# B's q by seven products per pair of row blocks, woven with B's k, with some bf16 sums on GpSimd

## The chip, the core and the metric

The kernel runs on one core of a Trainium2 chip. The core has TensorE (matrix products, PE in the profile; its weight loads are listed as PEld), VectorE (DVE), ScalarE (ACT), GpSimd (POOL) and SyncE (SP, which here issues the transfers). All work on SBUF, 128 partitions wide; TensorE writes to PSUM, whose banks serve as accumulators and hold 512 fp32 columns each. The metric is the device time of one execution in microseconds, here as the median of three runs: 192.18 us before.

## What is computed

Two linear-attention blocks, A and B, with their own weights, are applied to the same x and mixed by a gate of x. x is 2048 rows of 640 features, there are 32 heads of 20 features, everything is bf16.

```python
phi = lambda t: jnp.where(t > 0, t + 1, jnp.exp(t)) + 1e-6

def _A_ref(x, wqkv, wo):            # _B_ref is the same
    q, k, v = ...                   # x @ wqkv, split into heads
    pq, pk = phi(q), phi(k)
    kv = jnp.einsum("bhsd,bhse->bhde", pk, v)
    z = jnp.einsum("bhsd->bhd", pk)
    num = jnp.einsum("bhqd,bhde->bhqe", pq, kv)
    den = jnp.einsum("bhqd,bhd->bhq", pq, z)[..., None] + 1e-6
    return ... (num / den) @ wo

x = A_x
g = _sigmoid((x * gate_w).sum(-1, keepdims=True))
return g * _A_ref(x, A_wqkv, A_wo) + (1 - g) * _B_ref(x, B_wqkv, B_wo)
```

## The kernel before

Features are handled in five chunks of 128 (`DT`), rows in sixteen tiles of 128 (`ST`). `xn` holds x with rows on the partitions, `xT` x transposed; `pk` is phi(k) by rows, `pqT` phi(q) by features.

- **k.** `k_chunk` (L213) makes one row tile of phi(k): ten products of 320 columns into one accumulator of two banks (L205), then `phi` (L192): ScalarE takes the exponential (L195), VectorE clamps it in SBUF (L198) and takes the maximum with t + 1, read from the accumulator (L202).
- **q.** `q_unit` (L248) makes one feature chunk for 1024 rows: two times five products of 512 columns (L254), then `phi` on 1024 columns. With `lifted`, ScalarE also writes t + 1 to SBUF (L197), so that VectorE's maximum reads bf16 from SBUF only (L200).
- **G = x^T phi(k).** The fifth chunk of features runs directly (`g_pass`, L276, products at L288). The other four are done by seven products on 2 x 2 blocks (Strassen) in `g_strassen` (L320, products at L315). The sums of blocks that this needs are made by VectorE (`x_sum`, `k_sum`, all through L454).
- **KVT, M.** `kvt_pass` (L409) makes v's part from G, masked by head; `m_unit` (L417) multiplies it by wo, chunk by chunk, into `M`.
- **z and the denominators.** `z_rows` (L364) sums phi(k) over the rows, `z_pass` (L381) selects heads, `rec_pass` (L435) makes the gated reciprocals, `norm_spread` (L485) spreads them, and `scale` (L501) multiplies `pqT` with them.
- **Output.** pqT_A M_A + pqT_B M_B, again by seven products, for pairs of row tiles (`Pair`, L525, products at L515). VectorE makes the sums of blocks: `p_diff` (L456) writes D3, `p_sums` (L461) and `m_sums` (L472) the others, one line of `q_pass` makes TM0, the difference of M_A's halves.

The stages follow one another: A's k and q, A's G, B's k with A's KVT between, B's q, B's G, output. From the first G on, each engine works in the order in which the code is written (`tc.manual_schedule`); TensorE's first part is ordered by a planner. `ps` hands out four accumulators of two banks each in turn (`turn`), so a unit's accumulator is asked for again by the fourth unit after it. B's part stands in these lines:

```python
for i in range(ST):
    k_chunk(1, i)
    if i == 1:
        kvt_pass(0)
        wv[1] = load_w(1, "v", nc.sync)
    if i in (3, 6, 9, 12):
        r0 = (i - 3) // 3 * RB
        p_diff(slice(r0, r0 + RB))
...
zsel = q_pass(1, [(m, h) for h in range(2) for m in range(DT)])
load_wo(1, nc.sync)
g_all(1, zsel)
```

In `q_pass(1, ...)` z's rows, M's five units for A, two differences of k (`k_sum(1, 1)` and `k_sum(1, 2)`) and TM0 stand between the ten q units. GpSimd only builds masks and an identity in the first 10 us.

Of the kernel before, what the change touches and what calls it, by code (L numbers as in the profile page):

```python
# [8 lines left out]
P = 128  # L9
FP32 = mybir.dt.float32  # L10
# [21 lines left out]
def kernel(  # L32
# [19 lines left out]
    banks = ctx.enter_context(ExitStack())  # L52
    psum = banks.enter_context(tc.tile_pool(name="psum", bufs=1, space=bass.MemoryType.PSUM))

    turn = [0]

    def ps_raw(name, slot=None):

        if slot is None:
            slot = turn[0]  # L60
            turn[0] = (slot + 1) % 4
        return psum.tile([P, 4 * HB], BF16, tag=f"ps{slot}", name=name)
# [18 lines left out]
    R = persist.tile([P, 2, 4, RB], BF16, name="R")  # L81
    ones = persist.tile([P, H], BF16, name="ones")
    gwr = persist.tile([P, DT, H], BF16, name="gwr")
    D3 = persist.tile([P, DT, SH], BF16, name="D3")
# [6 lines left out]
    S3 = persist.tile([P, 3, hc, ic], BF16, name="S3")  # L91
    SX = {k: S3[:, k - 1] for k in (1, 2, 3)}
# [3 lines left out]
    lift = persist.tile([P, 1], FP32, name="lift")  # L96
    TM = [persist.tile([P, DT, HF], BF16, name="TM0")] + [None] * 3
    ge = [persist.tile([P, 2 * RB], FP32, name=f"ge{b}") for b in "AB"]
# [93 lines left out]
    def phi(dst, src, n, lifted=False):  # L192

        e = work.tile([P, 2, n], BF16, tag="e", name="e", bufs=3)
        nc.scalar.activation(out=e[:], in_=src, func=ACT.Exp)  # L195
        if lifted:
            nc.scalar.activation(out=dst, in_=src, func=ACT.Identity, bias=lift[:])  # L197
        nc.vector.tensor_scalar(e[:], e[:], 1.0, EPS, op0=ALU.min, op1=ALU.add)  # L198
        if lifted:
            nc.vector.tensor_tensor(out=dst, in0=dst, in1=e[:], op=ALU.max)  # L200
            return
        nc.vector.scalar_tensor_tensor(out=dst, in0=src, scalar=1.0 + EPS, in1=e[:], op0=ALU.add, op1=ALU.max)  # L202
# [7 lines left out]
    def k_done(b, i, pt):  # L210
        phi(pk[:, i, :].rearrange("p (b n) -> p b n", b=2), pt[:, :, 0:HF], HF)
# [36 lines left out]
    def q_unit(b, m, h, lifted=False):  # L248

        pt = ps(f"q{'AB'[b]}")  # L250
        for u in range(2):
            for c in range(DT):
                n = 2 * h + u
                nc.tensor.matmul(  # L254
                    pt[:, u, :], lhsT=mixed(wq[b][:, c, :], m), rhs=xT[:, c, n * HB:(n + 1) * HB],
                    start=(c == 0), stop=(c == DT - 1),
                )
        phi(pqT[b][:, m, h * 2 * HB:(h + 1) * 2 * HB].rearrange("p (b n) -> p b n", b=2), pt, HB, lifted)

    def q_block(b, m, n):  # L260

        pt = ps(f"q{'AB'[b]}")
        for u in range(2):
            for c in range(DT):
                nc.tensor.matmul(  # L265
                    pt[:, u, :], lhsT=mixed(wq[b][:, c, :], m + u), rhs=xT[:, c, n * HB:(n + 1) * HB],
                    start=(c == 0), stop=(c == DT - 1),
                )
        phi(pqT[b][:, m:m + 2, n * HB:(n + 1) * HB], pt, HB)
# [94 lines left out]
    def z_rows(b):  # L364

        pt = ps(f"z{'AB'[b]}")
# [7 lines left out]
        zr = work.tile([P, D], BF16, tag="zr", name="zr")  # L374
# [6 lines left out]
    def z_pass(b, zr):  # L381

        pt = ps(f"zs{'AB'[b]}")
# [8 lines left out]
    def kvt_mm(b, pt, hf):  # L392

        for j in range(4):
            for c in range(DT):
                nc.tensor.matmul(  # L396
                    pt[:KG, hf, j * KG:(j + 1) * KG], lhsT=wv[b][:, c, (4 * hf + j) * KG:(4 * hf + j + 1) * KG],
                    rhs=GT[hf][:, c, j * KG:(j + 1) * KG], start=(c == 0), stop=(c == DT - 1),
                )

    def kvt_mask(pt, hf):

        nc.vector.tensor_tensor(
            out=KVT[:KG, 2 * hf:2 * hf + 2, 0:3:2, :],
            in0=pt[:KG, hf, 0:HF].rearrange("p (g k n) -> p g k n", g=2, k=2),
            in1=maskE[:KG, None, None, :].to_broadcast([KG, 2, 2, KG]), op=ALU.mult,
        )

    def kvt_pass(b):  # L409

        pt = ps("kvA")
        for hf in range(2):
            kvt_mm(b, pt, hf)
        for hf in range(2):
            kvt_mask(pt, hf)
# [40 lines left out]
    def p_diff(rows):  # L456

        up = slice(SH + rows.start, SH + rows.stop)
        add_rows(D3[:, :, rows], pqT[0][:, :, rows], pqT[0][:, :, up], ALU.subtract)

# [64 lines left out]
    class Pair:  # L525
# [13 lines left out]
        def p1(self):  # L539
            prod(self.at("x"), pqT[0][:, :, 0:SH], M[0][:, :, 0:HF], self.i, True)  # L540
            self.p1s = work.tile([P, HF], FP32, tag="e", name="p1s", bufs=3)
            nc.scalar.copy(out=self.p1s[:], in_=self.at("x"))
# [12 lines left out]
        def p6(self):  # L555
            prod(self.at("x"), xT[:, :, 0:SH], TM[1], self.i, False)
            self.u2 = tmp("u2", "ex")
            nc.scalar.copy(out=self.u2[:], in_=self.at("x"))  # L558
            self.u3 = tmp("u3", "zr")
            out_add(self.u3[:], self.at("y"), self.u2[:])  # L560
# [39 lines left out]
    def q_pass(b, units):  # L600

        units = list(units)
        q_unit(b, *units.pop(0))
        if b == 0:
            gate_pass()
        zr = z_rows(b)
        if b == 1:
            m_unit(0, 0, "act")
        for k in range(2):
            if b == 0:  # L610
                x_sum(1 + k)
            q_unit(b, *units.pop(0), b == 0)
        zsel = z_pass(b, zr)
        for k, (m, h) in enumerate(units):
            if b == 0 and k < 2:
                if k:
                    x_sum(3)
                else:
                    k_sum(0, 2)
            q_unit(b, m, h, b == 0)  # L620
            if b == 1 and k in (0, 2):
                for c in range(k + 1, k + 3):
                    m_unit(0, c, "act")
            if b == 1 and k == 0:
                k_sum(1, 1)
            if b == 1 and k == 4:
                add_rows(TM[0][:], M[0][:, :, HF:D], M[0][:, :, 0:HF], ALU.subtract)
        if b == 1:
            k_sum(1, 2)
        return zsel  # L630

    def g_all(b, zsel):

        g_pass(b, DT - 1, 1)
        k_sum(b, 3)
        g_strassen(b, zsel)

# [3 lines left out]
    turn[0] = 2  # L641
    for n in range(2):
        for i in range(CB if n else 0, CB * 2 * n):
            k_chunk(0, i)
        for m in (0, 2):
            q_block(0, m, n)
    q_unit(0, DT - 1, 0)
    for i in range(hc, ST - 2):
        k_chunk(0, i)
# [10 lines left out]
    def late_pool(name):  # L660
        return tc.tile_pool(name=name, bufs=1, space=bass.MemoryType.PSUM, reuse_waits="tile")

# [3 lines left out]
    with tc.manual_schedule():  # L666
# [5 lines left out]
        zsel = q_pass(0, [(m, 1) for m in range(DT)])  # L672
        wq[1] = load_w(1, "q", nc.sync)
        g_all(0, zsel)

        turn[0] = 3
        for i in range(ST):
            k_chunk(1, i)
            if i == 1:
                kvt_pass(0)  # L680
                wv[1] = load_w(1, "v", nc.sync)
            if i in (3, 6, 9, 12):
                r0 = (i - 3) // 3 * RB
                p_diff(slice(r0, r0 + RB))
        t1 = wpool.tile([P, hc, HF], BF16, tag="wk", name="T1")
        TK[1][1] = t1[:]
        zsel = q_pass(1, [(m, h) for h in range(2) for m in range(DT)])
        load_wo(1, nc.sync)
        g_all(1, zsel)
        banks.close()  # L690
# [4 lines left out]
        part = [slice(n * RB, (n + 1) * RB) for n in range(4)]  # L695
# [3 lines left out]
        with late_pool("mid") as mid:  # L699
            first = bank(mid, "mid0", 2)  # L700
            kv = bank(mid, "mid1", 2)
            kvt_mm(1, kv, 0)
            kvt_mask(kv, 0)
            pairs[0].p1()
            kvt_mm(1, kv, 1)
            kvt_mask(kv, 1)
# [89 lines left out]
```

## Time and profile before

| | |
|---|---|
| median of three runs (lowest, highest) | 192.18 us (191.94, 192.31) |
| the profiled execution | 192.89 us, of which the profile's span is 191.1 |
| A's k and first q units, 10 to 41.5 us | 31.5 us |
| A's last q units and z, 41.5 to 57 us | 15.5 us |
| A's G, 57 to 74.1 us | 17.1 us |
| B's k and A's KVT, 74.1 to 97.4 us | 23.3 us |
| B's q, z and A's M, 97.4 to 123.8 us | 26.4 us |
| B's G, 123.8 to 145.1 us | 21.3 us |
| KVT, M and output, 145.1 us to the end | 46 us |

The page has these parts: busy time and share of the span of each engine; the span in 40 slices, a digit being the busy share in tenths; the chain that ended last, by engine; groups of instructions as "line engine operation out<-in xcount | busy us, mean ns | idle us before". In a timeline a row begins with its start and its length in us. In a table of windows a row gives the stretch, its length, then the busy us of PE, PEld, DVE, ACT and POOL (with counts), TensorE's granted clock, and the share and rate of the DMA engines. The granted clock is 1.00 in all of these stretches.

### The profile page before, as it was taken

What the parts mean: (1) busy time and instruction counts of PE and PEld (TensorE: products, weight loads), DVE (VectorE), ACT (ScalarE), POOL (GpSimd) and SP (SyncE); (2) the same over time, 40 slices, a digit from 0 to 9 for tenths busy, and PEclk for the clock granted to TensorE, in tenths of its full rate; (3) what the DMA queues carried; (4) which work ended last, traced back from release to release, by engine and by line L of the source; (5) the groups of instructions that cost most, each with busy time, mean ns of one, the idle gap of its engine ahead of it and who ended that gap; (6) DMA issues with size and microseconds to landing.
All of it is one profiled execution on the core that took longest, in us unless ns stands there. A gap on an engine that the chain in (4) does not pass through costs nothing.

```text
span 191.1 us, 3763 instructions
## 1 busy us (share of the span) xinstructions
PE 185.4 (97%) x1567; PEld 125.1 (65%) x1575; DVE 146.9 (77%) x236; ACT 74.0 (39%) x104; POOL 8.5 (4%) x23
## 2 busy tenths in 40 slices
PE   8799999999999999999999999999999999999993
PEld 3466657765577677877765555577677776777772
DVE  1378968899893997799985785895797989788554
ACT  2055446455942532254544545431621611111120
POOL 8900000000000000000000000000000000000000
PEclk9999999999999999999999999999999999999999
DMA  6976549981050000320000006100000002312222
GB/s 175 328 142 86 106 77 368 301 198 50 2 172 3 0 0 0 67 108 0 3 0 0 3 2 144 31 0 0 3 0 0 3 0 70 125 70 71 74 77 69
DMA packets 18879, 13.99 MB, mean 73 GB/s; under 512 B 9392, under 2 KB 18864, under 8 KB 18864
## 3 DMA queue, kind: packets, MB, share of 16 engines
q1 hardware_dynamic: 18288, 13.11, 26.0%
q10 hardware_dynamic: 576, 0.66, 1.0%
q8 instruction: 12, 0.20, 0.5%
q14 instruction: 3, 0.02, 0.0%
HBM read 9.18 MB, written 2.62 MB: 62 GB/s over the span
## 4 chain that ended last, share of the span: by engine, by line
PE 93%; DMA 3%; DVE 1%; ACTq 0%; issue 0%; ACT 0%; DVEq 0%
PE gs L315 16%; PE qB L254 11%; PE kB L205 11%; PE kA L205 11%; PE qA L254 7%; PE ox L515 6%; PE oy L515 5%; PE oz L515 5%; PE qA L265 4%; DMA xn<-in_A_x_dram 3%; PE ow L515 2%; PE gB L288 2%; PE gA L288 2%; PE mA L429 2%; DVE osb L520 1%; PE mid L396 1%
## 5 line engine op out<-in xcount | busy, mean ns | idle before, releaser
L205 PEld LDWEIGHTS <-xT 128*128 128x128 bf16 x320 | 31.0, 98 | 12.5 <-DVE xT L190 0.5
L198 DVE TENSOR_SCALAR e<-e 128x640 bf16<-128x640 bf16 (+1 forms) x52 | 18.8, 361 | 11.6 <-ACT e L195 11.1
L205 PE MATMUL kA<-wkA,xT 128*128 128x320 bf16 x160 | 22.6, 299 | 0.1
L254 PE MATMUL qB<-xT,wqB 128*128 128x512 bf16 x96 | 22.3, 380 | 0.2
L205 PE MATMUL kB<-wkB,xT 128*128 128x320 bf16 x160 | 22.1, 299 | 0.0
L254 PEld LDWEIGHTS <-wqB 128*128 128x128 bf16 x100 | 11.4, 118 | 9.7 <-issue 0.7
L195 ACT ACTIVATE e<-kB 128x640 bf16<-128x640 f32 x16 | 11.3, 704 | 14.2 <-PE kB L205 12.2
L195 ACT ACTIVATE e<-kA 128x640 bf16<-128x640 f32 x16 | 11.1, 704 | 13.8 <-PE kA L205 13.8
L195 ACT ACTIVATE e<-qB 128x1024 bf16<-128x1024 f32 x10 | 10.2, 1023 | 12.7 <-PE qB L254 12.7
L202 DVE SCALAR_TENSOR_TENSOR pk<-kA,e 128x640 bf16<-128x640 f32 x16 | 13.2, 825 | 1.7
L202 DVE SCALAR_TENSOR_TENSOR pk<-kB,e 128x640 bf16<-128x640 f32 x16 | 13.2, 825 | 1.7
L195 ACT ACTIVATE e<-qA 128x1024 bf16<-128x1024 f32 x10 | 10.2, 1023 | 10.6 <-PE qA L254 5.2
L254 PE MATMUL qA<-xT,wqA 128*128 128x512 bf16 x58 | 13.5, 380 | 0.1
L202 DVE SCALAR_TENSOR_TENSOR pqTB<-qB,e 128x1024 bf16<-128x1024 f32 x10 | 12.3, 1225 | 1.4 <-DVE e L198 0.5
L558 ACT COPY u<-ox 128x320 f32<-128x320 f32 x8 | 3.4, 425 | 21.9 <-PE ox L515 21.9
L315 PEld LDWEIGHTS <-S 128*128 128x128 bf16 x96 | 9.1, 98 | 4.2 <-issue 0.8
L315 PEld LDWEIGHTS <-xn 128*128 128x128 bf16 x96 | 9.4, 98 | 3.6
L254 PEld LDWEIGHTS <-wqA 128*128 128x128 bf16 x60 | 6.9, 118 | 5.6 <-issue 0.3
L515 PEld LDWEIGHTS <-xT 128*128 128x128 bf16 x85 | 8.0, 98 | 3.1 <-DVE xT L454 0.2
L515 PEld LDWEIGHTS <-pqTA 128*128 128x128 bf16 x85 | 7.9, 98 | 2.9 <-issue 0.2
L515 PEld LDWEIGHTS <-pqTB 128*128 128x128 bf16 x80 | 7.8, 98 | 3.0
L315 PE MATMUL gs<-pk,xn 128*128 128x320 bf16 x64 | 9.3, 299 | 0.0
(121 smaller groups left out, 280.4 us busy)
## 6 DMA issues: line engine op xcount, KB each, us to landing
out_dram<-osb SPq DMA_DIRECT2D x14, 160.0 KB, 1.8
xn<-in_A_x_dram SPq DMA_DIRECT2D x3, 640.0 KB, 6.2
wqA<-in_A_wqkv_dram SPq DMA_DIRECT2D x1, 800.0 KB, 6.4
wvA<-in_A_wqkv_dram SPq DMA_DIRECT2D x1, 800.0 KB, 9.9
woA<-in_A_wo_dram SPq DMA_DIRECT2D x1, 800.0 KB, 11.9
wkB<-in_B_wqkv_dram SPq DMA_DIRECT2D x1, 800.0 KB, 4.7
wqB<-in_B_wqkv_dram SPq DMA_DIRECT2D x1, 800.0 KB, 4.6
wvB<-in_B_wqkv_dram SPq DMA_DIRECT2D x1, 800.0 KB, 4.7
```

The costliest lines, as they stand in the source:

```text
L195: nc.scalar.activation(out=e[:], in_=src, func=ACT.Exp)
L198: nc.vector.tensor_scalar(e[:], e[:], 1.0, EPS, op0=ALU.min, op1=ALU.add)
L202: nc.vector.scalar_tensor_tensor(out=dst, in0=src, scalar=1.0 + EPS, in1=e[:], op0=ALU.add, op1=ALU.max)
L205: nc.tensor.matmul(pt[:, hf, 0:HF], lhsT=xT[:, c, i * P:(i + 1) * P], rhs=wk[b][:, c, hf * HF:(hf + 1) * HF], start=(c == 0), stop=(c == D ...
L254: nc.tensor.matmul(pt[:, u, :], lhsT=mixed(wq[b][:, c, :], m), rhs=xT[:, c, n * HB:(n + 1) * HB], start=(c == 0), stop=(c == DT - 1),)
L265: nc.tensor.matmul(pt[:, u, :], lhsT=mixed(wq[b][:, c, :], m + u), rhs=xT[:, c, n * HB:(n + 1) * HB], start=(c == 0), stop=(c == DT - 1),)
L288: nc.tensor.matmul(pt[:, hf, 0:HF], lhsT=xn[:, i, c * P:(c + 1) * P], rhs=pk[:, i, hf * HF:(hf + 1) * HF], start=(i == 0), stop=(i == ST - 1),
L315: nc.tensor.matmul(pt[:, n, 0:HF], lhsT=left[:, i, n * P:(n + 1) * P], rhs=right[:, i, :], start=(first and i == 0), stop=(i == hc - 1), s ...
L396: nc.tensor.matmul(pt[:KG, hf, j * KG:(j + 1) * KG], lhsT=wv[b][:, c, (4 * hf + j) * KG:(4 * hf + j + 1) * KG], rhs=GT[hf][:, c, j * KG:(j ...
L429: nc.tensor.matmul(dst[32 * g:32 * g + 32, :], lhsT=mixed(heads, c), rhs=wo_sb[b][:KG, 2 * g + k, hf * HF:(hf + 1) * HF], start=(k == 0), ...
L515: nc.tensor.matmul(dst, lhsT=left[:, c, r0:r0 + P], rhs=right[:, c, :], start=(first and c == 0), stop=(c == DT - 1), skip_group_check=not ...
L558: nc.scalar.copy(out=self.u2[:], in_=self.at("x"))
```

## The change

B's q is computed by seven products on 2 x 2 blocks. A block pair is (rows of block 2r, rows of block 2r + 1, 512 each) by (features m, m + 2), over the first four chunks of x in two pairs; the fifth chunk is multiplied directly. There are four such groups (m = 0, 1; r = 0, 1); the fifth feature chunk (`fifth`) is made as before. All seven products go into four banks: where Strassen's scheme adds two products, the second is accumulated onto the first, after ScalarE has copied, or VectorE has added, an accumulator into another.

```diff
+    def sq_sum(k, r):
+        lo, hi = [slice(n * HB, (n + 1) * HB) for n in (2 * r, 2 * r + 1)]
+        x11, x12, x21, x22 = [xT[:, c:c + 2, rows] for rows in (lo, hi) for c in (0, 2)]
+        a, b, op = {
+            1: (x21, x22, ALU.add), 2: (SQ[:, 0, r], x11, ALU.subtract),
+            3: (x11, x21, ALU.subtract), 4: (x12, SQ[:, 1, r], ALU.subtract),
+        }[k]
+        nc.gpsimd.tensor_tensor(out=SQ[:, k - 1, r], in0=a, in1=b, op=op)
+    def tq_sums(b):
...
+        for k, x, y in ((0, w12, w11), (1, w22, TQ[0]), (2, w22, w12), (3, w21, TQ[1])):
+            nc.gpsimd.tensor_tensor(out=TQ[k], in0=x, in1=y, op=ALU.subtract)
+    def q_strassen(b, m, r, quad, fills):
+        ce, cf, co, cz = quad
...
+        prod(ce, w_of(m), x_of(lo), (0, 1), True)
+        nc.scalar.copy(out=co, in_=ce)
+        a = work_of()
+        a.clamp()
+        a.top()
+        prod(cz, tq(1), sq(1), (0, 1), True)
+        p5 = work.tile([P, HB], FP32, tag="osb", name="p5", bufs=3)
+        nc.scalar.copy(out=p5[:], in_=cz)
+        prod(co, tq(2), sq(2), (0, 1), False)
+        add(cf, co, p5[:])
+        prod(ce, w_of(m), x_of(lo), (2, 3, 4), False)
+        f = Phi(pqT[b][:, m, rows(lo)], ce)
+        f.clamp()
+        f.top()
+        a = work_of()
+        a.clamp()
+        prod(co, tq(3), sq(3), (0, 1), False)
+        add(cz, co, p5[:])
+        a.top()
+        prod(cf, lambda c: natural(c + 2 * (c < 2), m + 2), lambda c: sq(4)(c) if c < 2 else x_of(lo)(c), (0, 1, 4), False)
+        f = Phi(pqT[b][:, m + 2, rows(lo)], cf)
+        f.clamp()
+        f.top()
+        a = work_of()
+        a.clamp()
+        a.top()
+        prod(co, lambda c: tq(4)(c) if c < 2 else natural(c, m), lambda c: x_of(hi)(c + 2 * (c < 2)), (0, 1, 4), False)
+        prod(cz, w_of(m + 2), x_of(hi), (4,), False)
+        f = Phi(pqT[b][:, m:m + 3:2, rows(hi)], [co, cz], True)
+        a = work_of()
+        f.clamp()
+        f.top()
+        if a is not None:
+            a.clamp()
+            a.top()
```

`Phi` is the old `phi` cut in two: making it issues ScalarE's part, `clamp` and `top` VectorE's two operations. `work_of` issues the next filler, mostly one k chunk of B. The loops around it:

```diff
+        for r in range(2):
+            for k in range(1, 5):
+                sq_sum(k, r)
-        zsel = q_pass(0, [(m, 1) for m in range(DT)])
+        zsel = q_pass([(m, 1) for m in range(DT)])
...
+        tq_sums(1)
+        new_stage("weave")
+        k_chunk(1, 0, 3)
+        k_chunk(1, 1, 2)
+        quad = [cell(f"q{n}", n)[:] for n in range(4)]
...
+        f = fifth(0, quad[1:3])
+        f.clamp()
+        f.top()
+        k_chunk(1, 2, 3)
+        fills = [chunk(3, 2), lambda: Masks(3)]
+        fills += [chunk(i, 2 + i % 2) for i in range(4, ST)]
+        fills.insert(13, lambda: fifth_two(1, 3))
+        fills[14:] = [chunk(ST - 1, 2), lambda: None]
+        for m, r in ((0, 0), (1, 0), (0, 1), (1, 1)):
+            q_strassen(1, m, r, quad, fills[:4])
+            fills = fills[4:]
...
+        k_sum(1, 1)
+        k_sum(1, 2)
+        load_wo(1, nc.sync)
+        new_stage("after")
+        g_pass(1, DT - 1, 0)
+        zr = z_rows(1, 1)
+        for c in range(DT):
+            m_unit(0, c, "act", ps("mA", (2, 3, 1)[c % 3]))
+        zsel = z_pass(1, zr, 2)
+        k_sum(1, 3)
+        part = [slice(n * RB, (n + 1) * RB) for n in range(4)]
+        nc.gpsimd.tensor_tensor(out=TM[0][:], in0=M[0][:, :, HF:D], in1=M[0][:, :, 0:HF], op=ALU.subtract)
+        for rows in part:
+            p_diff(rows)
+        g_strassen(1, zsel)
```

`Masks` is A's KVT as a filler. `p_diff` is the same subtraction on GpSimd, and runs beside B's G instead of between B's k chunks; TM0's difference goes to GpSimd too. In the weave two accumulators of two banks take the chunks in turn, beside the four banks of the group; then a third set of accumulators is laid out ("after"). Eight operand sums of 1024 elements (`sq_sum`) stand at the head of GpSimd's queue behind its masks, four of 512 (`tq_sums`) wait for B's q weights. D3 moves into the operand sums' tile `SQ`, the third sum of x goes into `xn` in place, and some small buffers share others. The first part of the kernel is put under `tc.manual_schedule`, which leaves TensorE's order there as it was.

More of the change, by code (lines that the diff above doesn't have):

```diff
@@ L51, with late_pool, new_stage, cell @@
     work = ctx.enter_context(tc.tile_pool(name="work", bufs=2))
-    banks = ctx.enter_context(ExitStack())
-    psum = banks.enter_context(tc.tile_pool(name="psum", bufs=1, space=bass.MemoryType.PSUM))
+    stage = []
+    def late_pool(name):
+        return tc.tile_pool(name=name, bufs=1, space=bass.MemoryType.PSUM, reuse_waits="tile")
+    def new_stage(name):
+        if stage:
+            stage.pop().close()
+        if name is not None:
+            held = ctx.enter_context(ExitStack())
+            stage.append(held)
+            pools["ps"] = held.enter_context(late_pool(name))
+    pools = {}
+    new_stage("first")
     turn = [0]
+    def cell(name, slot):
+        return pools["ps"].tile([P, HB], FP32, tag=f"cell{slot}", name=name)
     def ps_raw(name, slot=None):
@@ L246, in mixed, with q_mm @@
         return t[:, m::DT]
-    def q_unit(b, m, h, lifted=False):
-        pt = ps(f"q{'AB'[b]}")
-        for u in range(2):
-            for c in range(DT):
[L253 to L258, printed above, removed]
+    def q_mm(b, m, n, c, dst, first, last):
+        nc.tensor.matmul(
+            dst, lhsT=mixed(wq[b][:, c, :], m), rhs=xT[:, c, n * HB:(n + 1) * HB],
+            start=first, stop=last,
+        )
@@ L265, in q_block, with natural, x_of, prod @@
+    def q_strassen(b, m, r, quad, fills):
+        ce, cf, co, cz = quad
+        lo, hi = 2 * r, 2 * r + 1
+        fill = iter(fills)
+        def natural(c, t):
+            return mixed(wq[b][:, c, :], t)
+        def x_of(n):
+            return lambda c: xT[:, c, n * HB:(n + 1) * HB]
+        def prod(dst, left, right, cs, first):
+            for k, c in enumerate(cs):
                 nc.tensor.matmul(
-                    pt[:, u, :], lhsT=mixed(wq[b][:, c, :], m + u), rhs=xT[:, c, n * HB:(n + 1) * HB],
@@ L267, in q_block, with w_of, tq, sq @@
-                    start=(c == 0), stop=(c == DT - 1),
-                )
-        phi(pqT[b][:, m:m + 2, n * HB:(n + 1) * HB], pt, HB)
+                    dst, lhsT=left(c), rhs=right(c), start=first and k == 0, stop=k == len(cs) - 1,
+                    skip_group_check=not first,
+                )
+        def w_of(t):
+            return lambda c: natural(c, t)
+        def tq(k):
+            return lambda c: TQ[k - 1][:, c, m, :]
+        def sq(k):
+            return lambda c: SQ[:, k - 1, r, c, :]
@@ new lines, in rows, with add, work_of @@
+        def rows(n):
+            return slice(n * HB, (n + 1) * HB)
+        def add(dst, src, sb):
+            nc.vector.tensor_tensor(out=dst, in0=src, in1=sb, op=ALU.add)
+        def work_of():
+            return next(fill)()
+        prod(ce, w_of(m), x_of(lo), (0, 1), True)
[6 more added lines that the diff above has]
+        nc.scalar.copy(out=p5[:], in_=cz)
@@ L619, in q_pass @@
                     k_sum(0, 2)
[L620 to L629, printed above, removed]
-        return zsel
[L632 to L636, printed above, removed]
+            q_unit(0, m, h, True)
+        return zsel
     with tc.manual_schedule():
         k_first()
-    turn[0] = 2
-    for n in range(2):
-        for i in range(CB if n else 0, CB * 2 * n):
-            k_chunk(0, i)
[L645 to L649, printed above, removed]
+        turn[0] = 2
+        for n in range(2):
+            for i in range(CB if n else 0, CB * 2 * n):
+                k_chunk(0, i)
+            for m in (0, 2):
+                q_block(0, m, n)
+        q_unit(0, DT - 1, 0)
+        for i in range(hc, ST - 2):
+            k_chunk(0, i)
     with nc.allow_non_contiguous_dma(reason="640 elements, one to a partition and column"):
@@ L671 @@
         k_sum(0, 1)
-        zsel = q_pass(0, [(m, 1) for m in range(DT)])
+        for r in range(2):
+            for k in range(1, 5):
+                sq_sum(k, r)
+        zsel = q_pass([(m, 1) for m in range(DT)])
         wq[1] = load_w(1, "q", nc.sync)
[L674 to L680, printed above, removed]
-                wv[1] = load_w(1, "v", nc.sync)
-            if i in (3, 6, 9, 12):
-                r0 = (i - 3) // 3 * RB
-                p_diff(slice(r0, r0 + RB))
+        g_pass(0, DT - 1, 1)
@@ new lines, in fifth_two, with chunk, go, __init__ @@
+        def fifth_two(h, slot):
+            pt = ps("qB", slot)
+            return fifth(h, [pt[:, 0], pt[:, 1]])
+        def chunk(i, slot):
+            def go():
+                pt = ps("kB", slot)
+                for hf in range(2):
+                    for c in range(DT):
+                        k_mm(1, i, c, pt, hf)
+                return Phi(pk[:, i, :].rearrange("p (b n) -> p b n", b=2), pt[:, :, 0:HF])
+            return go
+        class Masks:
+            def __init__(self, slot):
+                self.pt = ps("kvA", slot)
+                for hf in range(2):
+                    kvt_mm(0, self.pt, hf, hf)
+                wv[1] = load_w(1, "v", nc.sync)
+            def clamp(self):
+                kvt_mask(self.pt, 0, 0)
+            def top(self):
+                kvt_mask(self.pt, 1, 1)
@@ L694 @@
         TM[1], TM[2] = t[:, 0], t[:, 1]
-        part = [slice(n * RB, (n + 1) * RB) for n in range(4)]
         half = ST // 2
```

142 lines of the change are left out of this document (84 added, 58 removed).

## The prediction

> **What bounds the kernel now.** I read the page's totals and slices first, then the chain of waits, then stage windows, then the timeline.
>
> ```profile
> PE 185.4 (97%) x1567; PEld 125.1 (65%) x1575; DVE 146.9 (77%) x236; ACT 74.0 (39%) x104; POOL 8.5 (4%) x23
> ...
> PE   8799999999999999999999999999999999999993
> ...
> DVE  1378968899893997799985785895797989788554
> ...
> POOL 8900000000000000000000000000000000000000
> ...
> PE 93%; DMA 3%; DVE 1%; ACTq 0%; issue 0%; ACT 0%; DVEq 0%
> ```
>
> TensorE is the bound from the second slice to the last; VectorE is close behind, and GpSimd is empty after its second slice. The windows, each row a stage with the busy us of each engine:
>
> ```profile
> 10.00:41.50 31.50, 31.34 (x196) 20.33 (x196) 25.70 (x43) 16.17 (x21) 0.00 (x0) 1.00 0.75 176
> ...
> 74.10:97.40 23.30, 23.30 (x203) 17.26 (x201) 19.55 (x37) 10.56 (x15) 0.00 (x0) 1.00 0.13 37
> 97.40:123.80 26.40, 26.19 (x215) 14.83 (x217) 19.35 (x26) 12.97 (x15) 0.00 (x0) 1.00 0.14 33
> 123.80:145.10 21.30, 21.30 (x193) 15.04 (x192) 17.59 (x16) 7.05 (x10) 0.00 (x0) 1.00 0.00 1
> ```
>
> The second row is B's k, the third B's q, the fourth B's seven products for G. The third number is TensorE: no gap to win in any of them, so only fewer products can help. The timeline shows what a chunk costs:
>
> ```profile
> 78.34 19.18 PE L205 MATMUL kB<-wkB,xT 128*128 128x320 bf16 x140
> ...
> 84.33 0.82 DVE L202 SCALAR_TENSOR_TENSOR pk<-kB,e 128x640 bf16<-128x640 f32 x1
> 85.07 0.32 DVE L198 TENSOR_SCALAR e<-e 128x640 bf16<-128x640 bf16 x1
> 85.33 0.70 ACT L195 ACTIVATE e<-kB 128x640 bf16<-128x640 f32 x1 [0.65 <-PE kB L205]
> 85.49 0.82 DVE L202 SCALAR_TENSOR_TENSOR pk<-kB,e 128x640 bf16<-128x640 f32 x1
> ```
>
> From one VectorE maximum to the next are 85.49 - 84.33 = 1.16 us a chunk. In the chain 140 chunk products take 19.02 us, 0.136 each (1.36 a chunk), and ten 512-wide ones 2.16, 0.216 each.
>
> **The change, part by part.**
>
> *Products.* B's q drops from 100 to 92 products of 512 columns (four groups of 18 for 20, twenty others kept); every other kind keeps its count. 8 x 0.216 = 1.73 us less TensorE, on the path: -1.73.
>
> *A group of the weave.* TensorE: 18 x 0.216 + 4 chunks x 1.36 = 9.32 us. VectorE: four chunks x 1.16; two clamp-and-maximum pairs of 512 columns, about 0.39 + 0.61 start to start (between the 640 and 1024 rows: 320 and 425 ns for the clamp, 825 and 1225 for the maximum); two sums of 512 written into an accumulator, 0.69 each, 0.61 start to start (rows: 489 ns for 320, 824 for 640, though none writes an accumulator); and for the upper half a clamp and a bf16 maximum of 1024 (425 and 693 ns, 1.14 start to start). 4.64 + 2.00 + 1.22 + 1.14 = 9.0. ScalarE: four exponentials of 704 ns, four of 512 columns (597 ns, L180's row), two lifts (about 0.65, from 1108 for 1024), two copies (about 0.58, between 425 for 320 and 677 for 640): 7.6. So TensorE still bounds, with 0.3 us to spare on VectorE, a thin cover.
>
> Two chains in a group can end later than TensorE arrives. First, the third small product may write its accumulator only when VectorE has read it for the sum. Counted from the end of the first chunk: result 0.24 later, exponential 0.70, VectorE's chunk 1.16, the sum 0.69, about 2.75; TensorE needs two short products, three more and a chunk, 4 x 0.216 + 0.65 + 1.36 = 2.87. It fits by 0.1. Second, at the border the copy into that accumulator stands on ScalarE behind two exponentials, two lifts and a chunk's exponential. ScalarE starts its next operation about 0.1 before the last ends (three of 704 in 1.90 us at 10.04), and then the copy is ready within 0.1 of its use; without that overlap each group waits 0.4. I take 0.1 a group, 0.3 us over the weave; the ends are 0 and 1.7.
>
> *After the weave.* The fifth feature's pass (32 x 0.136 = 4.36 us), z's rows (1.10) and M's five units (0.65 each) now follow one another instead of standing between q units. VectorE leaves the weave late: last product, 0.24, four ScalarE operations, the last pair: 3.5 us after TensorE. Then the two differences of k that stood in B's q stage, start to start 1.40 each: 6.3, and z's rows are read by 7.15. M's third unit takes that accumulator and wants it at 4.36 + 1.10 + 1.30 = 6.76: 0.4 us of wait. z's selection takes the accumulator of M's fourth unit, whose copy ends 0.20 + 0.70 after it, while the fifth unit covers 0.65: 0.3 more. Before, these sat in four rotating accumulators with q units between, and the timeline has no such wait. +0.7, ends 0 and 1.2.
>
> *Loads.* The load of B's wo moves behind M's last unit, from 115.24 to about 128 us; it lands 5.8 us after issue and is first used at 148.18, so it costs nothing with 14 us of cover. B's wv is again issued behind A's KVT products. Nothing else is queued behind either on SP until the stores at 158.97.
>
> *GpSimd.* It gets 8 sums of 1024 elements, 4 of 512, one of 1600, 4 of 1280 (the last two kinds taken off VectorE, 5 x 0.8 to 1.0 us that lay under TensorE). The trace has no two-input GpSimd operation. The nearest rows:
>
> ```profile
> L153 POOL TENSOR_SCALAR_AFFINE_SELECT E<-E 32x640 bf16<-32x640 bf16 x8 | 5.7, 712 | 0.4
> L454 DVE TENSOR_TENSOR D<-pqTA 128x1280 bf16<-128x1280 bf16 x4 | 3.3, 816 | 0.0
> ```
>
> One input costs GpSimd about 1.05 ns an element, so 1.1 us for 1024 is the lower bound; two inputs read in turn, 2.2 us, the upper. I take 2.1 ns an element. GpSimd is free from 9.72 us. The rows' sums can start when the transposed loads land: 15 issues in 21.08 us from 4.52, landing after 3.9 us, so the first four at 12.6 and the rest at 26.7; at 2.2 us each all are done by 36, and the weave reads them near 84. Weights land at 52.98 + 4.6 = 57.6, four sums end by 65. M's difference and D take 3.4 + 4 x 2.7 = 14.2 us from about 128, done at 142, first read at 150 and 153.8. Nothing late, cost 0, so long as they do not hold VectorE. The rows nearest to that are the E selects, which ran at 712 ns from 5.15 to 9.72 beside VectorE's copies; but those copies read an accumulator, and no row has both engines reading SBUF. I take side by side (0); the other end is the first rival.
>
> *Sum.* -1.73 + 0.3 + 0.7 = -0.7 us. The profiled execution took 192.89 (span 191.1 and 1.8 around it), 0.7 above the median of 192.18; so 192.2 for it, 191.5 on the median.
>
> **Rivals.**
>
> *GpSimd and VectorE take turns* whenever both read only SBUF. Place one, 13 to 22 and 27 to 36 us: each sum holds the next clamp, and VectorE's pair takes 2.2 + 0.1 + 0.32 = 2.6 instead of 1.16. A group of four sums makes it 5.8 late; the slack is 0.2 a k chunk and 0.5 a q unit, some 1.0 to 1.4 in all, and accumulators come round after three units (4.1 us, of which 2.1 are needed), 2.0: TensorE waits about 2.7, twice, 5.5. Place two, B's G stage: 14.2 us of GpSimd and VectorE's own SBUF work there (two k sums 2.9, five scales 5.8) make 22.9 in the 16.9 us from 128.2 to 145.1; the adds that free an accumulator stand behind the scales, so TensorE waits 6. Together 191.5 + 11.5 = 203; one place alone, 197. It decides from about 1.5 us a sum: at 1.1 us the pair takes 1.5 and place two sums to 15.7, and all is absorbed. For it: VectorE is at 82% in both places. Against it: no row shows such a hold.
>
> [...]
>
> *VectorE becomes the weave's bound.* If a sum into an accumulator takes the 640 row's 0.82, or ScalarE does not overlap, a group takes 9.7 to 9.9 instead of 9.4: four groups, +1.2 to +2, and the late VectorE adds to M's wait: 193 to 194.5. It decides from 0.3 us a group. For: 97% of VectorE. Against: the same rows packed well in B's k stage.
>
> *All waits hide*: -1.73, 190.4.
>
> *The products drop but the time does not*, because something else ends each stage: within 0.2% of 192.2. Against: TensorE is 100% in three of the four windows.
>
> **Numbers.** Forecast 0.42 (own range 190.4 to 192.6), turns 0.40, weave bound by VectorE 0.10, all hidden 0.06, no effect 0.02. About 0.2% (0.4 us) is what a measurement here can tell from none. Faster: 0.32 of the forecast's share and 0.06, 0.38. Same: 0.08 of it, 0.03 of turns with short sums, 0.02, 0.13. Slower: 0.02, 0.37 and 0.10, 0.49. The forecast is the likeliest single case; the range reaches from 190.3 into the turns case, to 203.5.
>
> **What would show it.** Right: 92 products of 512 columns in B's q, groups of 9.3 to 9.5 us, VectorE's clamps still 320 ns beside GpSimd's sums, M's third unit waiting 0.4. Wrong: gaps on TensorE near 17 to 24 and 31 to 38 us, clamps or scales starting as GpSimd sums end, or TensorE waiting for VectorE's sum inside each group.

## The result, and the profile after

The changed kernel takes 201.64 us (median of six runs, 201.03 to 202.13); the kernel before took 192.39 (191.94 to 193.57) beside it. The ratio is 1.047, with a 95% interval of 1.043 to 1.050: slower, where the prediction said 191.5 and a shade faster. The time lies inside the range, but only because the range reached into the rival in which GpSimd and VectorE take turns, whose price it is near.

From the page of the changed kernel: the totals, the slices, the clock in slices, and the chain by engine.

```profile
PE 187.6 (94%) x1567; PEld 125.5 (63%) x1567; DVE 160.4 (80%) x249; ACT 83.3 (42%) x130; POOL 48.2 (24%) x40
...
PE   8998898999999999999999999999919999999993
...
DVE  1399999999894997797989879469996789888644
...
POOL 8759479000008100000000000099940000000000
PEclk9999999999999999999999999999975999999999
...
PE 64%; DVE 26%; issue 3%; DMA 2%; ACT 2%; ACTq 0%; DVEq 0%
```

VectorE's share of the chain that ended last rose from 1% to 26%. TensorE's holes, in slices 4, 5, 7 and 30 of about 5 us each, lie where GpSimd is busy (3 to 7 and 27 to 30; slices 13 and 14, with the sums of wq, have none), and the clock falls to a half behind the last. The waits of TensorE between 10 and 156 us (what waited, for whom, us in total, times, longest):

```profile
PE gs L448 <- DVE GT L465: 4.4, 1, 4.4
PE kA L247 <- DVE pqTA L238: 2.0, 3, 0.7
PE kA L247 <- DVE pk L238: 0.7, 2, 0.4
PE zsB L518 <- ACT MA L407: 0.3, 1, 0.3
PE qA L291 <- DVE pk L238: 0.2, 1, 0.2
PE mA L554 <- DVE zr L508: 0.2, 1, 0.2
```

None of them lies in the weave. The time went to two places, and the weave gave a little back. In stages, from the start of the first product of each in the profiled executions:

| stage | before | after | difference |
|---|---|---|---|
| start to A's first q product | 12.29 | 11.42 | -0.87 |
| from there to B's first k product | 61.81 | 65.64 | +3.83 |
| from there to B's seven products for G | 54.05 | 52.69 | -1.36 |
| the seven products | 16.96 | 23.55 | +6.59 |
| the rest | 45.99 | 46.50 | +0.51 |
| span | 191.1 | 199.8 | +8.70 |

The first row is not part of the change. It follows the landing of x's first tiles, for which a transpose on TensorE waited 1.14 us in the one execution and 0.32 in the other, and it lies between 11.15 and 12.50 us in the profiled executions of all versions below. The second row is steady: the kernel before, and each of the four versions below that has no sum of x on GpSimd, takes 61.80 or 61.81 us there. So the first place cost 3.83 us. The list of waits shows 2.9 of them; the rest stands in TensorE's busy time in this stretch, 62.77 us in place of 61.60.

The first place, in the timeline of the changed kernel (start and length in us first), and behind it the clamp's group in the kernel before (busy us, mean ns):

```profile
15.44 2.12 POOL L322 TENSOR_TENSOR SQ<-SQ,xT 128x1024 bf16<-128x1024 bf16 x1
15.60 2.25 DVE L229 TENSOR_SCALAR e<-e 128x1024 bf16<-128x1024 bf16 x1
...
17.52 2.30 POOL L322 TENSOR_TENSOR SQ<-xT 128x1024 bf16<-128x1024 bf16 x1
17.95 1.23 DVE L238 SCALAR_TENSOR_TENSOR pqTA<-qA,e 128x1024 bf16<-128x1024 f32 x1
...
19.09 1.02 DVE L229 TENSOR_SCALAR e<-e 128x1024 bf16<-128x1024 bf16 x1
19.23 1.52 PE L247 MATMUL kA<-wkA,xT 128*128 128x320 bf16 x10 [0.61 <-DVE pqTA L238]
```

```profile
L198 DVE TENSOR_SCALAR e<-e 128x1024 bf16<-128x1024 bf16 x20 | 8.5, 425 | 8.3 <-ACT e L195 8.3
```

VectorE's clamp of 1024 elements took 0.43 us in the kernel before. Here it takes 2.25 and 1.02, and ends some 0.3 us after the GpSimd sum beside it (15.44 + 2.12 = 17.56 against 17.85; 17.52 + 2.30 = 19.82 against 20.11). VectorE is never shown idle meanwhile: a held instruction appears as a long one, not as a wait. The maximum, which reads the accumulator and one tile in SBUF, keeps its 1.23 us in the middle of a sum. The second place, in the changed kernel and then, where it matters, in the kernel before:

```profile
130.25 4.48 POOL L851 TENSOR_TENSOR TM<-MA 128x1600 bf16<-128x1600 bf16 x1 [64.33 <-ACT MA L407]
134.70 12.52 POOL L584 TENSOR_TENSOR SQ<-pqTA 128x1280 bf16<-128x1280 bf16 x4
...
135.87 1.75 DVE L574 RECIPROCAL rT<-d 128x256 bf16<-128x256 f32 x1
137.54 3.68 DVE L579 TENSOR_TENSOR xT<-pk,xT 128x2560 bf16<-128x2560 bf16 x1
141.14 7.16 DVE L631 TENSOR_TENSOR pqTB<-pqTB,R 128x2048 bf16<-128x2048 bf16 x2
148.22 0.81 DVE L465 TENSOR_TENSOR GT<-gs,u 128x640 bf16<-128x640 f32 x1
148.95 3.48 DVE L631 TENSOR_TENSOR pqTB<-pqTB,R 128x2048 bf16<-128x2048 bf16 x3
...
149.08 4.42 PE L448 MATMUL gs<-pk,MB 128*128 128x320 bf16 x16 [4.39 <-DVE GT L465]
```

```profile
135.93 1.43 DVE L454 TENSOR_TENSOR xT<-pk,xT 128x2560 bf16<-128x2560 bf16 x1
...
138.73 2.36 DVE L504 TENSOR_TENSOR pqTB<-pqTB,R 128x2048 bf16<-128x2048 bf16 x2 [1.37 <-ACT R L496]
...
142.93 2.34 PE L315 MATMUL gs<-pk,MB 128*128 128x320 bf16 x16
```

Two scales take 7.16 us (2.36 before) while GpSimd makes D, and a sum of k 3.68 (1.43); the three behind them, after GpSimd ended at 147.22, take 3.48. The add that frees TensorE's accumulator stands behind the first two, TensorE waits 4.39 us for it, and the 16 products that follow take 4.42 us at a granted clock of 0.50 (from 149 to 153 us), about twice the 2.34 that 16 such products take earlier in the stage and took before. The reciprocal, which reads and writes SBUF only, keeps the 1.75 us it had before.

### The profile page after: what moved, and what is told of

Its sections match the earlier page's. It is cut to its first block, busy times and chain, and to the rows that moved or that the text cites. A ratio compares the mean times of both kernels' runs of the same rounds, so it can differ in the third digit from the quotient of the medians.

```text
span 199.8 us, 3829 instructions
## 1 busy us (share of the span) xinstructions
PE 187.6 (94%) x1567; PEld 125.5 (63%) x1567; DVE 160.4 (80%) x249; ACT 83.3 (42%) x130; POOL 48.2 (24%) x40
## 4 chain that ended last, share of the span: by engine, by line
PE 64%; DVE 26%; issue 3%; DMA 2%; ACT 2%; ACTq 0%; DVEq 0%
PE gs L448 11%; PE kB L247 10%; DVE e L229 7%; PE q L345 7%; DVE pk L238 6%; PE qA L291 5%; PE ox L642 5%; PE oy L642 5%; PE oz L642 5%; DVE pqTA L238 3%; DVE xT L579 3%; DVE pqTB L631 2%; PE ow L642 2%; DMA xn<-in_A_x_dram 2%; PE gA L421 2%
## 5 line engine op out<-in xcount | busy, mean ns | idle before, releaser
L229 DVE TENSOR_SCALAR e<-e 128x640 bf16<-128x640 bf16 (+2 forms) x56 | 26.7, 477 | 6.1 <-ACT e L224 5.7
L291 PE MATMUL qA<-xT,wqA 128*128 128x512 bf16 x100 | 22.4, 379 | 0.2 <-DVE pk L238 0.2
L851 POOL TENSOR_TENSOR TM<-MA 128x1600 bf16<-128x1600 bf16 x1 | 4.5, 4482 | 64.3 <-ACT MA L407 64.3
L291 PEld LDWEIGHTS <-wqA 128*128 128x128 bf16 x100 | 11.6, 118 | 9.7 <-issue 0.7
L224 ACT ACTIVATE e<-qA 128x1024 bf16<-128x1024 f32 x10 | 10.2, 1024 | 11.0 <-PE qA L291 10.8
L224 ACT ACTIVATE e<-q 128x512 bf16<-128x512 f32 x18 | 10.8, 598 | 5.0 <-PE q L345 3.4
L584 POOL TENSOR_TENSOR SQ<-pqTA 128x1280 bf16<-128x1280 bf16 x4 | 12.5, 3159 | 0.0
L448 PE MATMUL gs<-pk,MB 128*128 128x320 bf16 x32 | 6.8, 384 | 4.4 <-DVE GT L465 4.4
L669 ACT COPY p1s<-ox 128x320 f32<-128x320 f32 x8 | 3.4, 426 | 17.7 <-PE ox L642 17.7
L322 POOL TENSOR_TENSOR SQ<-xT 128x1024 bf16<-128x1024 bf16 x4 | 8.9, 2224 | 7.7 <-DMA xT<-in_A_x_dram 7.7
L631 DVE TENSOR_TENSOR pqTB<-pqTB,R 128x2048 bf16<-128x2048 bf16 x5 | 10.6, 2173 | 0.0
```

The costliest lines, as they stand in the source:

```text
L224: nc.scalar.activation(out=to, in_=part, func=ACT.Exp)
L229: nc.vector.tensor_scalar(self.e, self.e, 1.0, EPS, op0=ALU.min, op1=ALU.add)
L291: nc.tensor.matmul(dst, lhsT=mixed(wq[b][:, c, :], m), rhs=xT[:, c, n * HB:(n + 1) * HB], start=first, stop=last,)
L322: nc.gpsimd.tensor_tensor(out=SQ[:, k - 1, r], in0=a, in1=b, op=op)
L448: nc.tensor.matmul(pt[:, n, 0:HF], lhsT=left[:, i, n * P:(n + 1) * P], rhs=right[:, i, :], start=(first and i == 0), stop=(i == hc - 1), s ...
L584: nc.gpsimd.tensor_tensor(out=D3[:, :, rows], in0=pqT[0][:, :, rows], in1=pqT[0][:, :, up], op=ALU.subtract)
```

## The experiments

Theory T: a GpSimd sum and a VectorE operation with all its operands in SBUF never run side by side; each waits for the whole instruction of the other. So worded, T is too wide, as the reciprocal shows; what the traces show held are the clamps, sums and scales. The rivals were that the new order of the code causes the lateness, and that the two engines share a rate.

**The sums on VectorE, the weave kept.** `p_diff` too goes through `add_rows`, which is VectorE's. The copy of one element holds the sums of wq back.

```
-        nc.gpsimd.tensor_tensor(out=SQ[:, k - 1, r], ...)
+        nc.vector.tensor_tensor(out=SQ[:, k - 1, r], ...)
...
+        if b == 0:
+            for k in range(1, 5):
+                sq_sum(k, 0)
         rts = rec_pass(b, zsel, 2)
...
-        for r in range(2):
-            for k in range(1, 5):
-                sq_sum(k, r)
...
+        nc.gpsimd.tensor_copy(out=TM[0][0:1, 0, 0:1], in_=SQ[0:1, 3, 0, 0, 0:1])
         tq_sums(1)
         new_stage("weave")
+        sq_sum(1, 1)
+        sq_sum(2, 1)
         k_chunk(1, 0, 3)
         k_chunk(1, 1, 2)
+        sq_sum(3, 1)
...
         k_chunk(1, 2, 3)
+        sq_sum(4, 1)
...
         zr = z_rows(1, 1)
+        part = [slice(n * RB, (n + 1) * RB) for n in range(4)]
+        for rows in part[:3]:
+            p_diff(rows)
...
         k_sum(1, 3)
+        p_diff(part[3])
+        add_rows(TM[0][:], ...)
```

> Same weave and same seven products; the eight sums of x run on VectorE (four in the 2.95 us in which it waits for A's denominator, four beside B's first k chunks), the four D sums and TM0 too (three in the 2.56 us before zsel, the rest in the 1.68 us before B's denominator); only the four sums of wq stay on GpSimd, held back until VectorE's sums are done. Theory T (a GpSimd sum and a VectorE operation whose operands all lie in SBUF take whole turns): both stretches come back to the times of before, clamps of 0.32 and 0.42 us, two scales 2.36 us, and the 1.38 us of the weave stay: 190.9 us, between 190.4 and 191.6. Rival R2 (the lateness comes from the new order of the code: the k sums behind the weave, the adds into accumulators): B's G stage stays 6 us late and the time is 198 us or more.

Measured: 190.62 us (190.33 to 190.88) against 191.88 before, a ratio of 0.9933 (0.9916 to 0.9951). Stages in the profiled execution, as in the table above and from A's first q product on: 61.80, 52.62, 16.96, 45.92. Its windows of A's k and q, the weave and B's seven products (columns as in the table of windows above):

```profile
10.00:41.00 31.00, 30.84 (x192) 19.96 (x192) 25.67 (x43) 15.72 (x21) 0.00 (x0) 1.00 0.75 178
73.60:113.60 40.00, 39.74 (x271) 25.52 (x274) 36.36 (x69) 26.09 (x44) 0.00 (x0) 1.00 0.07 22
126.20:143.20 17.00, 17.00 (x166) 11.95 (x164) 15.30 (x15) 5.66 (x8) 0.00 (x0) 1.00 0.23 49
```

Both late stretches are gone and the gain of the weave stays; this version is faster than both kernels. On VectorE the eight sums cost some 0.61 us each start to start, and four of them lie in a wait that was there anyway:

```profile
57.20 0.68 DVE L322 TENSOR_TENSOR SQ<-xT 128x1024 bf16<-128x1024 bf16 x1
...
59.12 0.68 DVE L322 TENSOR_TENSOR SQ<-xT,SQ 128x1024 bf16<-128x1024 bf16 x1
60.24 0.42 DVE L572 SCALAR_TENSOR_TENSOR d<-denA,geA 128x256 f32<-128x256 f32 x1 [0.43 <-PE denA L192]
```

**One place at a time.** The two halves of that edit, each alone and at the same places in the code.

```
-        nc.gpsimd.tensor_tensor(out=D3[:, :, rows], ...)
+        add_rows(D3[:, :, rows], ...)
...
-        nc.gpsimd.tensor_tensor(out=TM[0][:], ...)
+        add_rows(TM[0][:], ...)
```

> As the changed kernel, but D's four sums and TM0 run on VectorE; the eight sums of x stay on GpSimd. T: B's G stage takes 17 us again in place of 23.6, the A phase stays 3 us late: 194.1 us (193.4 to 194.8). R2: 201 us.

```
-        nc.gpsimd.tensor_tensor(out=SQ[:, k - 1, r], ...)
+        nc.vector.tensor_tensor(out=SQ[:, k - 1, r], ...)
```

> As the changed kernel, but the eight sums of x run on VectorE; D's four sums and TM0 stay on GpSimd. T: the A phase comes back by 3.0 us, B's G stage stays 6.7 us late: 198.5 us (197.8 to 199.3). R2: 201 us.

Measured: 194.85 us (ratio 1.017, 1.013 to 1.021) and 197.56 us (1.029, 1.025 to 1.034). With D back on VectorE, B's seven products take 16.96 us; with the sums of x back, the stretch from A's first q product to B's first k product takes 61.81 us, as before, and the seven products 23.57. So each place goes with its own GpSimd sums, and the rival of the code's order, which both kernels keep, falls. Both medians lie just outside their ranges, on either side. The expectations had taken the first place as 3 us; with 3.83 the second version should take 201.64 - 3.83 = 197.8, which it does within 0.3. The first place has no fixed price: with D back the profiled execution was the slowest of its four, the stretch took 67.42 us (65.64 in the changed kernel), the first sum began 0.64 us after A's first q product (0.98 in the changed kernel), two clamps of 640 were held for 2.1 us each, and TensorE waited 4.5 us for VectorE in place of 2.9.

**Shorter sums, still on GpSimd.**

```
+        for c in range(2):
+            for n in range(2):
+                cut = slice(n * 2 * P, (n + 1) * 2 * P)
+                nc.gpsimd.tensor_tensor(out=SQ[:, k - 1, r, c, cut], in0=a[:, c, cut], in1=b[:, c, cut], op=op)
...
+        for c in range(DT):
+            nc.gpsimd.tensor_tensor(out=D3[:, c, rows], ...)
...
+        for c in range(DT):
+            nc.gpsimd.tensor_tensor(out=TM[0][:, c], ...)
```

> As the changed kernel, every sum still on GpSimd, but in pieces: each sum of x in four of 256 elements, each D sum in five of 256, TM0 in five of 320. T: a VectorE operation waits for the piece that is running and no longer, so no clamp lasts over 1.2 us (1.0 to 2.3 us in the changed kernel) and the two scales that took 7.16 us take under 4; B's G stage loses 0.5 to 2 us in place of 6.65: 194 to 198 us. Rival R1 (the two engines share a rate, so that the same bytes cost the same whatever the length of the instructions): the stretches stay as late as they are, 201 to 202 us.

Measured: 193.15 us (1.008, 1.005 to 1.011), better than T's 194 to 198 and far from the 201 of a shared rate. Stages: 62.21, 52.68, 16.96, 47.90. In its timeline:

```profile
15.03 0.59 DVE L229 TENSOR_SCALAR e<-e 128x1024 bf16<-128x1024 bf16 x1
...
16.86 0.82 DVE L229 TENSOR_SCALAR e<-e 128x1024 bf16<-128x1024 bf16 x1
...
128.85 18.74 POOL L588 TENSOR_TENSOR SQ<-pqTA 128x256 bf16<-128x256 bf16 x20
...
136.63 3.10 DVE L635 TENSOR_TENSOR pqTB<-pqTB,R 128x2048 bf16<-128x2048 bf16 x2 [1.37 <-ACT R L627]
139.65 0.81 DVE L468 TENSOR_TENSOR GT<-gs,u 128x640 bf16<-128x640 f32 x1
140.38 4.80 DVE L635 TENSOR_TENSOR pqTB<-pqTB,R 128x2048 bf16<-128x2048 bf16 x3
...
146.44 0.93 PE L532 MATMUL mid<-GT,wvB 128*80 128x80 bf16 x20 [1.83 <-DVE KVT L539]
```

The same elements in pieces (0.67 us for the first of 256) hold a clamp by 0.1 to 0.4 us, and the slack swallows nearly all of that: 0.40 us are lost between A's first q product and B's first k product, nothing in the seven products. What is left is one wait further on: three scales held to 4.80 us (3.49 in the version without D on GpSimd) push the mask of B's KVT back, and TensorE waits 1.83 us for it. The clamps of the changed kernel, which end some 0.3 us after the sums, and this run fit turns of whole instructions and not a shared rate.

**The hold without the change.** Eight useless differences of x, or eight fills, put into the kernel before.

```
+        dump = S3[:].rearrange("p k i n -> p (k i n)")
+        for r in range(2):
+            ...
+            for k, (a, b) in enumerate(((x21, x22), (x21, x11), (x11, x21), (x12, x11))):
+                nc.gpsimd.tensor_tensor(out=dump[...], in0=a, in1=b, op=ALU.subtract)
```

> The kernel before, with nothing of the change in it, plus eight GpSimd differences of 1024 elements a partition of the same parts of x, written to a buffer that x's own sums overwrite later; nobody reads them. T (whole turns): clamps of 1 to 2 us in the two stretches from 13 to 22 and from 26 to 36 us, and the A phase 3 us late, nothing else: 195.0 us (194.2 to 195.8). Rival R3 (the A phase is late because the changed kernel puts its first part into a fixed order, or because of its pools): 192 us, clamps of 0.32 and 0.42 us.

```
+            nc.gpsimd.tensor_tensor(out=dump[0:1, 0:2]..., in0=xT[...], in1=xT[...], op=ALU.add)
+            for k in range(4):
+                nc.gpsimd.memset(dump[:, k * 1024:k * 1024 + 2048], 0.0)
```

> The kernel before plus eight GpSimd fills with zero (2048 elements, about 2.0 us each by the 0.64 us of the one of 640), held back by a sum of one element to the same two stretches; nobody reads them. T, form one (a clamp waits for any GpSimd instruction that uses SBUF): clamps of 1 to 2 us, 195 us as with the sums. T, form two (it waits only where GpSimd reads SBUF): clamps keep 0.32 and 0.42 us, 192 us.

Measured: 195.93 us with the sums (1.020, 1.018 to 1.022) and 193.23 with the fills (1.007, 1.004 to 1.010), against 192.14. With the sums only the stretch from A's first q product to B's first k product is late (65.28 us in place of 61.81; the three stages behind it are 54.06, 16.96 and 45.99), as T has it; the median lies a little above T's range, which ended at 195.8. So the hold needs neither the order nor the buffers of the changed kernel. From the timelines, first of the sums, then of the fills:

```profile
15.87 2.24 DVE L198 TENSOR_SCALAR e<-e 128x1024 bf16<-128x1024 bf16 x1
18.22 1.22 DVE L202 SCALAR_TENSOR_TENSOR pqTA<-qA,e 128x1024 bf16<-128x1024 f32 x1
...
20.48 1.22 DVE L202 SCALAR_TENSOR_TENSOR pqTA<-qA,e 128x1024 bf16<-128x1024 f32 x1
```

```profile
13.81 7.83 POOL L679 MEMSET S<- 128x2048 bf16 x4
...
14.78 1.18 DVE L198 TENSOR_SCALAR e<-e 128x1024 bf16<-128x1024 bf16 x1
16.06 1.23 DVE L202 SCALAR_TENSOR_TENSOR pqTA<-qA,e 128x1024 bf16<-128x1024 f32 x1
...
18.08 1.23 DVE L202 SCALAR_TENSOR_TENSOR pqTA<-qA,e 128x1024 bf16<-128x1024 f32 x1
```

A fill, which reads nothing, holds the clamp too: form one is right in the mechanism and wrong in its price, 195. The rhythm fits the prices, though no run varies it alone. Under the hold VectorE does one clamp and one maximum for each GpSimd instruction: the maxima start 2.26 us apart beside the sums (18.22 to 20.48) and 2.02 apart beside the fills (16.06 to 18.08), while TensorE's unit of ten 512-wide products takes 2.16. The first rhythm is slower than TensorE's, the second is not. With the fills the stretch takes 62.97 us, 1.16 more than before, and the median is up by as much (1.09); with the sums it was 3.47. Where the 1.16 come from stays open. B's first k product stands at 74.28 us with the fills, only 0.2 later than before, because that execution reached A's first q product 0.98 us earlier.

**Plain products, woven the same way.**

```
-        prod(ce, w_of(m), x_of(lo), (0, 1), True)
...
+        every = range(DT)
+        prod(ce, w_of(m), x_of(lo), every, True)
...
+        prod(cf, w_of(m + 2), x_of(lo), every, True)
...
+        prod(co, w_of(m), x_of(hi), every, True)
...
+        prod(cz, w_of(m + 2), x_of(hi), every, True)
```

> As the version with the sums on VectorE, same stages and the same weaving with k chunks, but each group of q makes its four blocks by 20 plain products in place of 18 by Strassen, and the sums of x and wq and the adds between accumulators are left out; the output is the reference's. If the gain comes from the eight products saved (8 x 0.216 = 1.73 us): 192.3 us (191.8 to 192.7), no better than the kernel before. If it comes from weaving q with k: 190.6 us.

Measured: 192.09 us (1.000, 0.998 to 1.001); the stage from B's first k product to the seven products takes 53.88, against 52.62 with Strassen and 54.05 before. The weaving alone brings nothing that can be measured. The eight products bring 1.26 us in the stage, of their 1.73, and as much in the whole time: each version against the kernel before beside it, 0.9999 - 0.9933 = 0.0066 of 192 us, 1.27. (The medians differ by 1.47, but the kernel before was itself 0.26 slower beside this version than beside the other, 192.14 against 191.88.) With Strassen the fifth feature's pass behind the weave starts some 0.3 us after the last q product should end, and M's five units take 3.19 us in place of 2.94.

**The wait filled.** On the version with only the sums of x on VectorE.

```
+        if b == 1:
+            idle = ps("idle", 3)
+            for k in range(16):
+                nc.tensor.matmul(idle[:, 0, :], lhsT=one_l, rhs=one_r, start=True, stop=True)
         g_prod(even, SX[4], b22, False)
```

> As the version with only the sums of x on VectorE (D and TM0 on GpSimd, TensorE idle for 4.4 us and then 16 products in 4.43 us at a granted clock of 0.50), plus 16 products of 512 columns on constants that nobody reads, in that wait. If the lower clock follows from TensorE's idle time: the 16 products behind take 2.2 us at a clock of 1.00 and the stage 21.3 us in place of 23.6: 194.3 to 196.3 us. If it follows from the turns of GpSimd and VectorE: still 4.4 us, 197.6 us.

Measured: 196.32 us against 197.56 without them, at the edge of the forecast. Timeline:

```profile
141.56 3.66 PE L499 MATMUL idle<-const-bfloat16-1.0 128*128 128x512 bf16 x15
146.11 2.33 PE L448 MATMUL gs<-pk,MB 128*128 128x320 bf16 x16 [0.88 <-DVE GT L465]
...
150.70 0.93 PE L536 MATMUL mid<-GT,wvB 128*80 128x80 bf16 x20 [0.82 <-DVE KVT L543]
```

The 16 products take 2.33 us in place of 4.43, and the stage 21.50 in place of 23.57, though VectorE's add comes as late as without the filling (they start 4.38 us after the end of the stage's products ahead of them, 146.11 against 139.39 + 2.34; 4.40 without), and the granted clock is 1.00 from 142 to 148 us: the half clock went with TensorE's idle time, 4.40 us there and 0.88 here. Of the 2.07 us, 0.82 go to the next wait, on VectorE, which the slow products had hidden. The gain in the whole time is less sure: of the four executions without the products two took 198.52 us, the profiled one among them, and two 196.37 and 196.59, these with a mean clock of 0.991 in place of 0.98. Against the latter two, 196.32 is no gain.

## Why the prediction was wrong

**The step that failed** is the GpSimd one: "Nothing late, cost 0, so long as they do not hold VectorE", and then "I take side by side". The durations of the sums of x in it were right: 1024 elements took 2.12 to 2.31 us (2.1 to 2.3 ns an element, for the 2.1 taken). M's difference and D took 4.48 + 12.52 = 17.0 us for the 14.2 forecast, and ended at 147.22 for 142. No reader waited for a sum. But the sums held VectorE's clamps, sums and scales, and TensorE waited for these: +3.83 and +6.59 us where the prediction has 0. (Its lower bound of 1.05 ns an element should be 1.11, 712 ns for 640; the sum does not use it.) The nearest row, the E selects beside VectorE's copies from an accumulator, could not decide it, as the text itself said; the maximum, which also reads an accumulator, indeed runs beside a sum in its usual 1.23 us. So "side by side" was an estimate of the author's that no row of the profile before showed, and 2.25 us for a clamp of 0.43 is what the changed kernel showed.

**The rival of turns** had the mechanism, the two places and nearly the total (203). Of its sizes, place one, 5.5, measured 3.83: it took the pair of a k chunk, 1.16 us made 2.6, for every sum, while five of the eight sums held the clamp of a q unit, where the held pair comes every 2.26 us against TensorE's 2.16, and three the clamp of a chunk (1.32, 0.92 and 0.92 us). In the profiled execution with D back on VectorE four clamps of chunks were held (2.12, 2.14, 1.72 and 1.36 us), and the stretch lost 5.61. This suggests that the number of k chunks met sets the price; it is not shown. Place two, 6, measured 6.59, but of other parts: a wait of 4.39, and 2.1 us because 16 products then ran at half clock, which no term had. That the 6 came so near is luck. The sums were not shared out as it had them either: at 130.18 VectorE's k sum went first, and GpSimd's of 1600 elements took 4.48 us for the 3.4 it was given.

**Products**, -1.73: in the changed kernel the stage got 1.36 shorter, with the waits below inside; 1.27 between the versions with and without Strassen, each against the kernel before beside it.

**The weave**, +0.3, and the rival in which VectorE bounds it: no TensorE wait in it. From one group to the next are 9.32 us (91.59, 100.91 and 110.23 in the chain of the changed kernel), the 18 x 0.216 + 4 x 1.36 of the text. (The text's 0.24 us from a last product to its result is some 0.19 in the kernel before: the ten products from 74.10 end at 75.46 by 0.136 each, and ScalarE starts at 75.65.) VectorE was busy for 8.35 and 8.40 us of the two stretches between these starts. The version with the sums on VectorE put two more sums, 1.22 us start to start, into the first part of the weave and TensorE still waited for nothing there, which suggests a thicker cover than the 0.3 us counted.

**After the weave**, +0.7: M's third unit waits 0.2 for z's accumulator where 0.4 was forecast, z's selection 0.3 as forecast. **Loads**: nothing waits for wo or wv.

**The sum**, -0.7, is what the change should bring if nothing holds VectorE. The nearest run, the version with the sums on VectorE, is 1.26 us faster than the kernel before (191.88 - 190.62), so the sum without the failed term gave some 0.6 us too little.

## What to carry to other kernels

A sum moved to an idle GpSimd was not free here: beside it VectorE's clamps (0.43 us became up to 2.25), sums of k (1.43 became 3.68) and scales (two took 7.16 in place of 2.36) were held. Price such a sum as a hold of the whole GpSimd instruction, and ask whether VectorE's rhythm under the hold is still faster than TensorE's unit. Here VectorE made the same sum in 0.61 us that GpSimd made in 2.2, and had idle stretches, before a denominator and before a first chunk, in which it cost nothing. If a sum must go to GpSimd, cut it into short instructions, which lost 1.3 us here (193.15 against 191.88) where the long ones lost 9.3, or put it beside reciprocals (1.75 us) and maxima read from an accumulator (1.23), which were not held.

## What the hardware showed unexpectedly

- An instruction that waits for the other engine's turn appears as a longer busy one (0.43 us became 2.25), so VectorE's busy time rose and its idle time did not; only the mean duration against that of the kernel before gives the hold away.
- A write-only fill on GpSimd holds VectorE's clamp as a sum does (1.18 us for 0.43; whether it holds a VectorE operation with two inputs in SBUF was not run), while reciprocals keep their 1.75 us (in the changed kernel at 64.16 beside a sum of wq, at 133.80 and 135.87 beside M's difference and D).
- About 3 us after TensorE fell idle, its granted clock went to a half and stayed there for nearly 7 us. In the version with D on GpSimd and the sums of x on VectorE:

```profile
144.00:145.00 1.00, 0.00 (x0) 0.00 (x0) 1.00 (x1) 0.00 (x0) 0.40 (x1) 0.82 0.00 0
145.00:146.00 1.00, 0.00 (x0) 0.00 (x0) 1.00 (x2) 0.00 (x0) 0.00 (x0) 0.50 0.00 0
...
151.00:152.00 1.00, 1.00 (x19) 0.92 (x18) 0.74 (x3) 0.00 (x0) 0.00 (x0) 0.77 0.00 0
152.00:153.00 1.00, 1.00 (x20) 0.84 (x19) 0.37 (x1) 0.42 (x1) 0.00 (x0) 1.00 0.00 0
```

The last products before it end near 141.9 us; the clock, the third number from the right, is 0.82 in the window from 144, 0.77 in that from 151 and 1.00 again from 152, so it fell near 144.6 and rose near 151.5. A wait of 4.4 us so cost 6.5. The fall came about 2.8 us after the last products' end, and the return some 5 us after the products began again at 146.27. In the changed kernel the products end at 144.70, the clock is 0.91 in the window from 147 and 0.50 in that from 148: a fall after about 3.1 us.
